# A fused attention, gated MLP and Fourier-mixing kernel: two weight tiles moved among the first q/k tiles, small additions moved to ScalarE

## The chip, the cores and the metric

The kernel runs as one program on one NeuronCore of a Trainium2 chip. The metric is device time in microseconds (us) of one execution; runs are summed up by their median. TensorE is PE in the profile, VectorE is DVE, ScalarE is ACT, GpSimd is POOL and SyncE is SP.

## The reference

The inputs are q, k and v of 4 batches with 8 heads, 512 local and 32 global tokens, and the weights of two MLPs. Each local query sees the 32 global keys and the local keys up to 32 tokens away; each global query sees all keys. Then a gated MLP with a convolution over 3 tokens follows, a Fourier transform over tokens and features, a normalisation, and a second MLP.

```python
def _attn_ref(q_l, k_l, v_l, q_g, k_g, v_g):
    def sm(s):
        s = s - np.max(s, axis=-1, keepdims=True)
        e = np.exp(s)
        return e / (np.sum(e, axis=-1, keepdims=True) + 1e-09)
    ...
    s_g = scale * np.matmul(q_g, k_all.transpose(0, 1, 3, 2))
    out_g = np.matmul(sm(s_g), v_all)
    ...
    s_l = np.concatenate([s_lg, s_ll], axis=-1)
    a_l = sm(s_l)
    out_l = np.matmul(a_l, np.concatenate([v_g, v_l], axis=2))
    return np.concatenate([out_g, out_l], axis=2).astype(np.float32)

def _moe_ref(x, w_in, conv_w, w_out):
    h = np.maximum(x @ w_in, 0.0)
    ...
    gate = 1.0 / (1.0 + np.exp(-conv_out))
    return (h * gate @ w_out).astype(np.float32)

def _moe2_ref(x, w_ch1, w_ch2):
    X = np.fft.fft(np.fft.fft(x, axis=1), axis=2)
    u = x + np.real(X).astype(np.float32)
    ...
    return (u + np.maximum(un @ w_ch1, 0.0) @ w_ch2).astype(np.float32)
```

## The kernel before

The attention goes in 32 units (`for i in range(NU + 2)`), each two heads of one batch and one half of the local queries. A unit's steps are spread over three turns of the loop. In turn i: `s_mm(i)` is eight matmuls for the scores into two banks; `s_max(i)` (L311) adds the mask and takes the row maximum, four DVE instructions with an accumulator read each; `s_exp(i)` (L323) is four exponentials on ScalarE, each with the row sums as its accumulated output in `sm[:, 4:8]`; `s_norm(i)` adds 1e-9 to the four sums (L328), inverts them (L329), and POOL scales the four blocks (L334). In turn i+1 `t_mm` transposes the blocks on PE (L344, L345) and `t_evac` copies them out (L353), half on DVE, half on ScalarE; in turn i+2 `pv_mm` multiplies with v. Units 0 to 3 are the second half of batch 0, units 4 to 7 the first. In turns 5 and 7 of each eight a global softmax stands beside them (`sg_piece`, `pg_soft`, `pg_trans`): two reductions L405, one exponential L415, addition L416, reciprocal L417, scaling on POOL L418, transposes L428 and L429.

The MLP's weights are given as 64-bit floats. For each of 16 tiles (w0 to w7 of the first matrix, w8 to w15 of the second, each 512 KB) `fetch_w` loads the raw words and `make_w` turns them into a pair of 32-bit parts. `from_f64` takes the magnitude on ScalarE (L167), clamps it on POOL (L168), shifts the tail either on ScalarE (L170) or on DVE (L172), and joins the words on DVE (L174, L175). `put` casts on ScalarE (L203) and subtracts on DVE (L204). There are two `mag` buffers, so a third tile waits until the first one's L204 has read its own. The tiles are loaded and made in the order `wq` = w0, w1, w8, w2, w9, w3 and so on; `wsteps` says how many are made in each turn. The first MLP's matmuls begin in turn 6 (`m_g1`).

On SP and PE the order is the program's own (`manual_schedule`). On DVE, ScalarE and POOL the instructions are ordered by the framework's scheduler, with the priorities in `PRIORITY`; a conversion may be issued only after the instruction kept in `last_exp` (`issue_after`). The first weight load has an explicit wait for the matmul `first`. The transfers on SP's queue share eight semaphores in turn, so each waits until the one eight places before it has landed.

Of the kernel before, what the change touches and what calls it, by code (L numbers as in the profile page):

```python
# [128 lines left out]
def fused_kernel(ctx: ExitStack, tc: tile.TileContext, d, out):  # L129
# [186 lines left out]
    @prio("ex")  # L316
    def s_exp(i):
        sm = smalls[i]
        for h in range(2):
            for a in range(2):  # L320
                k = 2 * h + a
                p = pbs(i)[h][:, a, 0:224]
                last_exp[0] = act.activation(p, p, AF.Exp, bias=sm[:, k:k + 1], scale=-1.0, accum_out=sm[:, 4 + k:5 + k])  # L323

    @prio("no")
    def s_norm(i):
        sm = smalls.pop(i)
        dve.tensor_scalar(sm[:, 8:12], sm[:, 4:8], 1e-9, None, op0=ALU.add)  # L328
        dve.reciprocal(sm[:, 12:16], sm[:, 8:12])  # L329
        for h in range(2):  # L330
            for a in range(2):
                p = pbs(i)[h][:, a, 0:224]
                k = 12 + 2 * h + a
                gp.tensor_scalar(p, p, sm[:, k:k + 1], 1.0, op0=ALU.mult, op1=ALU.mult)  # L334
# [76 lines left out]
    def pg_soft(g):  # L411
# [3 lines left out]
        act.activation(s, s, AF.Exp, bias=sm[:, 2:3], scale=-1.0, accum_out=sm[:, 3:4])  # L415
        dve.tensor_scalar(sm[:, 4:5], sm[:, 3:4], 1e-9, None, op0=ALU.add)  # L416
        dve.reciprocal(sm[:, 5:6], sm[:, 4:5])  # L417
# [40 lines left out]
    @prio("w")  # L458
    def make_w(i):
        w = put(wp, f"w{i}", unpack(mp, w_raw.pop(i), gp, i % 2 == 0))  # L460
        (w_in if i < 8 else w_out)[i % 8] = w
# [81 lines left out]
    with tc.manual_schedule(engines={mybir.EngineType.SP, mybir.EngineType.PE}):  # L543
        load_qk(0)
        sp.dma_start(mask[:, 2:4], d["mask"][:, 2:4])
        load_qk(1)
        sp.dma_start(ident, d["ident"])
        load_qk(2)
        for t in pbuf:
# [11 lines left out]
        wq = [0] + [x for m in range(7) for x in (m + 1, 8 + m)] + [15]  # L561
        wsteps = [0, 1, 2, 4, 6, 8, 10, 12, 14, 16]
        fetched = 0
        craw = ap1.tile([128, 24, 2], I32, name="craw")
        cmag = ap1.tile([128, 24], F32, name="cmag")
        for i in range(NU + 2):
# [4 lines left out]
            if live:  # L571
                first = s_mm(i, ("s", "t") if not early or i % 2 == 0 else ("a0", "a1"))
                if i == 0:
                    fetch_w(wq[0], first)
                    load_v(0)
                    sp.dma_start(mask[:, 0:2], d["mask"][:, 0:2])
                    fetched = 1
                while fetched < min(16, (2, 4, 7, 10, 13, 16)[min(i, 5)]):
                    fetch_w(wq[fetched])
                    fetched += 1  # L580
                if i == 1:
                    sp.dma_start(craw.rearrange("p a b -> p (a b)"), bits(d["conv_w"]))
                    gp.dma_start(gmask, d["gmask"])
                s_max(i)
            m_tanh(us[0] - 1)
            if 0 <= i - 2 < NU:
# [395 lines left out]
```

## Time and profile before

| | |
|---|---|
| Runs | 797.38, 797.80, 799.71 us; median 797.8 |
| Profiled execution | 796.53 us; its span 794.6 us |
| PE busy | 765.2 us (96%) |
| DVE busy | 477.9 us (60%) |
| ScalarE busy | 365.1 us (46%) |
| POOL busy | 159.2 us (20%) |
| Moved by the DMA queues | 77.80 MB, mean 98 GB/s |

The span is the time between the first and the last instruction in the trace; the 1.9 us around it belong to the execution's own time. Busy shares are means over stages that differ: in the first 40 us the DMA engines move 311 and then 401 GB/s and PE is little more than half busy; from some 70 us on PE is busy nearly without a gap.

### The profile page before, as it was taken

Reading aid. Unit: us, or ns where it says so; the run is one execution under the profiler, and the core shown is the slowest. Engines: PE = TensorE matmul, PEld = TensorE weight load, DVE = VectorE, ACT = ScalarE, POOL = GpSimd, SP = SyncE. Lnnn points to the kernel's source line nnn. Section 1 sums busy time; section 2 is a strip of 40 time slices with the busy share of each in tenths; the row PEclk is TensorE's granted clock in tenths of the full one; section 3 lists DMA queues with packets and bytes.
Section 4 is the critical chain, followed back from the end, with each engine's and each line's share of the span. In section 5 each row is a group of like instructions: output and inputs, shape, how many; then the busy total and the mean of one; then the engine's idle time right before and its main releaser. Section 6 shows DMA issues by size and latency. Waiting matters only on the chain.

```text
span 794.6 us, 13609 instructions
## 1 busy us (share of the span) xinstructions
PE 765.2 (96%) x5272; PEld 704.4 (89%) x5272; DVE 477.9 (60%) x1167; ACT 365.1 (46%) x884; POOL 159.2 (20%) x213
## 2 busy tenths in 40 slices
PE   6589999999999999999999999999999999999997
PEld 4368989998999988899889999999999999999997
DVE  6999787778777877699775778535422232213113
ACT  6787776777677775545533384313122112211110
POOL 5644423222322221000222022100022012100000
PEclk9889999999999999999999999999999999999999
DMA  8913423442345233436530670020200020001001
GB/s 310 401 45 108 141 79 126 135 168 79 127 134 169 78 111 107 115 114 234 182 102 1 225 254 1 1 91 0 66 26 2 1 90 1 1 1 45 1 1 45
DMA packets 36944, 77.80 MB, mean 98 GB/s; under 512 B 3768, under 2 KB 22072, under 8 KB 36880
## 3 DMA queue, kind: packets, MB, share of 16 engines
q1 hardware_dynamic: 36288, 74.52, 27.0%
q0 software_dynamic: 592, 2.42, 1.2%
q8 instruction: 41, 0.67, 0.3%
q14 instruction: 23, 0.19, 0.1%
HBM read 61.72 MB, written 15.20 MB: 97 GB/s over the span
## 4 chain that ended last, share of the span: by engine, by line
PE 85%; DVE 7%; DMA 3%; ACT 3%; issue 1%; POOL 1%; SPq 0%; DVEq 0%; POOLq 0%; ACTq 0%
PE ps_a L146 34%; PE ps_g L146 23%; PE ps_pv L146 15%; PE ps_s L146 6%; PE ps_t L146 3%; DMA qk<-in_qk_dram 2%; PE ps_s L344 1%; PE ps_t L344 1%; PE ps_s L345 1%; PE ps_t L345 1%; DMA uc<-u_d 1%; ACT pb L323 1%; DVE uc L857 1%; DVE cf L854 1%; DVE mag L174 1%
## 5 line engine op out<-in xcount | busy, mean ns | idle before, releaser
L146 PE MATMUL ps_a<-g,w_w 128*128 128x254 f32 (+1 forms) x768 | 112.7, 295 | 0.2 <-DVE u L541 0.2
L146 PE MATMUL ps_g<-x,w_w 128*128 128x256 f32 (+1 forms) x768 | 111.0, 293 | 1.1 <-ACT h L479 1.1
L146 PEld LDWEIGHTS ps_g<-x,w_w 128*128 128x128 f32 x768 | 100.3, 188 | 6.6 <-issue 4.4
L146 PEld LDWEIGHTS ps_a<-g,w_w 128*128 128x128 f32 x768 | 100.8, 190 | 4.5 <-issue 3.8
L146 PE MATMUL ps_a<-hd,w_w 128*128 128x436 f32 (+1 forms) x480 | 101.4, 360 | 0.0
L334 POOL TENSOR_SCALAR pb<-pb,sm 128x224 f32<-128x224 f32 x128 | 76.1, 613 | 109.2 <-DVE sm L329 42.3
L146 PEld LDWEIGHTS ps_a<-hd,w_w 128*128 128x128 f32 x480 | 90.1, 188 | 4.8
L826 DVE SCALAR_TENSOR_TENSOR hd<-ps_g,hd 128x436 fp32r<-128x436 f32 (+1 forms) x40 | 24.3, 608 | 88.7 <-ACT hd L825 88.7
L168 POOL TENSOR_SCALAR mag<-mag 128x512 f32<-128x512 f32 x48 | 39.6, 827 | 185.0 <-ACT mag L167 183.6
L146 PE MATMUL ps_a<-hd,w_v 128*128 128x436 f32 (+1 forms) x360 | 76.2, 360 | 0.0
L826 DVE SCALAR_TENSOR_TENSOR hd<-ps_pv,hd 128x436 fp32r<-128x436 f32 (+1 forms) x40 | 24.2, 605 | 85.1 <-ACT hd L825 85.1
L825 ACT ACTIVATE hd<-ps_pv 128x436 fp32r<-128x436 f32 (+1 forms) x40 | 21.3, 533 | 115.0 <-PE ps_pv L146 115.0
L825 ACT ACTIVATE hd<-ps_g 128x436 fp32r<-128x436 f32 (+1 forms) x40 | 21.3, 534 | 110.1 <-PE ps_g L146 110.0
L146 PEld LDWEIGHTS ps_a<-hd,w_v 128*128 128x128 f32 x360 | 67.6, 188 | 3.7
L323 ACT ACTIVATE pb<-pb,sm 128x224 f32<-128x224 f32 x128 | 60.4, 473 | 10.6 <-DVE sm L311 10.3
L490 DVE SCALAR_TENSOR_TENSOR y<-h,convw,y 128x254 f32<-128x254 f32 (+1 forms) x64 | 33.7, 527 | 29.0 <-ACT y L489 29.0
L146 PE MATMUL ps_g<-chl,w_w 128*128 128x436 f32 (+1 forms) x240 | 51.0, 361 | 0.0
L146 PE MATMUL ps_s<-qk 64*128 64x224 f32 (+1 forms) x144 | 38.3, 418 | 13.1 <-DMA qk<-in_qk_dram 8.0
L146 PE MATMUL ps_pv<-chl,w_v 128*128 128x436 f32 (+1 forms) x240 | 50.8, 360 | 0.0
L146 PE MATMUL ps_pv<-chl,w_w 128*128 128x436 f32 (+1 forms) x240 | 50.8, 360 | 0.0
L146 PEld LDWEIGHTS ps_pv<-chl,w_v 128*128 128x128 f32 x240 | 45.1, 188 | 2.5
L146 PEld LDWEIGHTS ps_g<-chl,w_w 128*128 128x128 f32 x240 | 44.8, 188 | 2.7 <-issue 0.3
(221 smaller groups left out, 1422.5 us busy)
## 6 DMA issues: line engine op xcount, KB each, us to landing
v<-in_v_dram SPq DMA_DIRECT2D x16, 640.0 KB, 4.9
qk<-in_qk_dram SPq DMA_DIRECT2D x16, 464.0 KB, 5.3
raw_r<-in_ch_dram SPq DMA_DIRECT2D x14, 512.0 KB, 6.2
raw_v<-in_ch_dram SPq DMA_DIRECT2D x13, 512.0 KB, 9.4
kept<-w_o SPq DMA_DIRECT2D x12, 512.0 KB, 3.8
w_w<-kept SPq DMA_DIRECT2D x12, 512.0 KB, 4.4
qk<-in_qk_dram SPq DMA_DIRECT2D x16, 304.0 KB, 4.9
u_d<-u SPq DMA_DIRECT2D x4, 1088.0 KB, 5.2
```

What stands on the lines that cost most here:

```text
L146: return pe.matmul(o, a, b, start=start, stop=stop)
L168: (clamp or dve).tensor_scalar(mag, mag, TOP, 2.0, op0=ALU.min, op1=ALU.max)
L174: dve.scalar_tensor_tensor(val, val, 3, tail, op0=ALU.logical_shift_left, op1=ALU.bitwise_or)
L323: last_exp[0] = act.activation(p, p, AF.Exp, bias=sm[:, k:k + 1], scale=-1.0, accum_out=sm[:, 4 + k:5 + k])
L334: gp.tensor_scalar(p, p, sm[:, k:k + 1], 1.0, op0=ALU.mult, op1=ALU.mult)
L344: pe.transpose(tb[:, 128 * a:128 * a + 128], pb[:, a, 0:128], ident)
L345: pe.transpose(tb[:, 256 + 128 * a:384 + 128 * a], pb[:, a, 128:256], ident)
L490: dve.scalar_tensor_tensor(y, hb[:, cc - 1:cc - 1 + n], convw2[:, m, 0:1], y, op0=ALU.mult, op1=ALU.add)
L825: act.activation(hd[:, 0], o, AF.Relu)
L826: dve.scalar_tensor_tensor(hd[:, 1], o, 0.0, f32(hd[:, 0]), op0=ALU.max, op1=ALU.subtract)
L854: dve.tensor_mul(tmp[:, e], acc[e], rs_t[c])
L857: dve.tensor_add(o, o, tmp[:, e])
```

## The change

The change does five things.

1. The loads of q/k tiles 1 and 2 and of the identity move behind unit 0's scores in the program, and w0 and w1 are loaded among them: w0 ahead of q/k tile 1, w1 ahead of q/k tile 2. w0's load loses its wait for the matmul.
2. w0 is made in turn 0, right behind `s_max(0)`, without the `issue_after`; `wsteps` is moved accordingly, so one more tile is made by the end of turns 0 to 5 (two more in turn 1), and the same number from turn 6 on.
3. w0's tail is shifted on DVE (L172) and no longer on ScalarE (L170).
4. The addition of 1e-9 to a unit's sums is a Copy with a bias on ScalarE (L324 of the changed kernel), issued behind the four exponentials, and it is what `last_exp` keeps.
5. The same for the global softmax (L416).

```diff
--- before.py
+++ after.py
@@ -320,12 +320,12 @@
             for a in range(2):
                 k = 2 * h + a
                 p = pbs(i)[h][:, a, 0:224]
-                last_exp[0] = act.activation(p, p, AF.Exp, bias=sm[:, k:k + 1], scale=-1.0, accum_out=sm[:, 4 + k:5 + k])
+                act.activation(p, p, AF.Exp, bias=sm[:, k:k + 1], scale=-1.0, accum_out=sm[:, 4 + k:5 + k])
+        last_exp[0] = act.activation(sm[:, 8:12], sm[:, 4:8], AF.Copy, bias=1e-9)
 
     @prio("no")
     def s_norm(i):
         sm = smalls.pop(i)
-        dve.tensor_scalar(sm[:, 8:12], sm[:, 4:8], 1e-9, None, op0=ALU.add)
         dve.reciprocal(sm[:, 12:16], sm[:, 8:12])
         for h in range(2):
             for a in range(2):
@@ -413,7 +413,7 @@
         s = sg4s[g % 2][:, 0:KC]
         dve.tensor_tensor(sm[:, 2:3], sm[:, 0:1], sm[:, 1:2], op=ALU.min)
         act.activation(s, s, AF.Exp, bias=sm[:, 2:3], scale=-1.0, accum_out=sm[:, 3:4])
-        dve.tensor_scalar(sm[:, 4:5], sm[:, 3:4], 1e-9, None, op0=ALU.add)
+        act.activation(sm[:, 4:5], sm[:, 3:4], AF.Copy, bias=1e-9)
         dve.reciprocal(sm[:, 5:6], sm[:, 4:5])
         gp.tensor_scalar(s, s, sm[:, 5:6], 1.0, op0=ALU.mult, op1=ALU.mult)
 
@@ -457,7 +457,7 @@
 
     @prio("w")
     def make_w(i):
-        w = put(wp, f"w{i}", unpack(mp, w_raw.pop(i), gp, i % 2 == 0))
+        w = put(wp, f"w{i}", unpack(mp, w_raw.pop(i), gp, i % 2 == 0 and i > 0))
         (w_in if i < 8 else w_out)[i % 8] = w
 
     g_t, acc = {}, {}
@@ -543,9 +543,6 @@
     with tc.manual_schedule(engines={mybir.EngineType.SP, mybir.EngineType.PE}):
         load_qk(0)
         sp.dma_start(mask[:, 2:4], d["mask"][:, 2:4])
-        load_qk(1)
-        sp.dma_start(ident, d["ident"])
-        load_qk(2)
         for t in pbuf:
             dve.memset(t[:, :, 224:256], 0.0)
         for t in sg4s:
@@ -559,7 +556,7 @@
         NU = B * H
         glob = {8 * b + 5 + 2 * k: 2 * b + k for b in range(B) for k in range(2)}
         wq = [0] + [x for m in range(7) for x in (m + 1, 8 + m)] + [15]
-        wsteps = [0, 1, 2, 4, 6, 8, 10, 12, 14, 16]
+        wsteps = [1, 2, 4, 5, 7, 9, 11, 12, 14, 16]
         fetched = 0
         craw = ap1.tile([128, 24, 2], I32, name="craw")
         cmag = ap1.tile([128, 24], F32, name="cmag")
@@ -571,10 +568,14 @@
             if live:
                 first = s_mm(i, ("s", "t") if not early or i % 2 == 0 else ("a0", "a1"))
                 if i == 0:
-                    fetch_w(wq[0], first)
+                    fetch_w(wq[0])
+                    load_qk(1)
+                    sp.dma_start(ident, d["ident"])
+                    fetch_w(wq[1])
+                    load_qk(2)
                     load_v(0)
                     sp.dma_start(mask[:, 0:2], d["mask"][:, 0:2])
-                    fetched = 1
+                    fetched = 2
                 while fetched < min(16, (2, 4, 7, 10, 13, 16)[min(i, 5)]):
                     fetch_w(wq[fetched])
                     fetched += 1
@@ -582,6 +583,8 @@
                     sp.dma_start(craw.rearrange("p a b -> p (a b)"), bits(d["conv_w"]))
                     gp.dma_start(gmask, d["gmask"])
                 s_max(i)
+                if i == 0:
+                    make_w(wq[0])
             m_tanh(us[0] - 1)
             if 0 <= i - 2 < NU:
                 pv_mm(i - 2, "pv" if not early or (i - 2) // 2 % 2 == 0 else "g1")
```

What the order of instructions shows. SP's queue from its start (`raw_w0` is the raw tile of w0, and so on), before and then now:

```order
L273 DMA qk_103<-in_qk_dram 128x608
L545 DMA mask_86<-in_mask_dram 128x448
L273 DMA qk_106<-in_qk_dram 128x608
L547 DMA ident_85<-in_ident_dram 128x128
L273 DMA qk_109<-in_qk_dram 128x608
L182 DMA raw_w0_135<-in_w_in_dram 128x4x256
L280 DMA v_137<-in_v_dram 128x1280
L576 DMA mask_86<-in_mask_dram 128x448
L182 DMA raw_w1_140<-in_w_in_dram 128x4x256
```

```order
L273 DMA qk_103<-in_qk_dram 128x608
L545 DMA mask_86<-in_mask_dram 128x448
L182 DMA raw_w0_130<-in_w_in_dram 128x4x256
L273 DMA qk_132<-in_qk_dram 128x608
L573 DMA ident_85<-in_ident_dram 128x128
L182 DMA raw_w1_135<-in_w_in_dram 128x4x256
L273 DMA qk_137<-in_qk_dram 128x608
L280 DMA v_139<-in_v_dram 128x1280
L577 DMA mask_86<-in_mask_dram 128x448
```

w0 stands ahead of the second q/k tile, w1 ahead of the third; both v and the second half of the mask come behind all of them.

DVE from its first waiting instruction on (`pb` and `sm` are a unit's block and its row statistics), before and then now:

```order
L311 ISA pb0_90,sm_142<-ps_s_129,mask_86 128x224
L311 ISA sm_142 128x1
L311 ISA pb0_90,sm_142<-ps_s_129,mask_86 128x224
L311 ISA sm_142 128x1
L311 ISA pb1_91,sm_142<-ps_t_130,mask_86 128x224
L311 ISA sm_142 128x1
L311 ISA pb1_91,sm_142<-ps_t_130,mask_86 128x224
L311 ISA sm_142 128x1
L328 TENSOR_SCALAR sm_142<-sm_142 128x4
L329 RECIPROCAL sm_142<-sm_142 128x4
```

```order
L172 TENSOR_SCALAR raw_w0_130<-raw_w0_130 128x512
L311 ISA pb0_90,sm_142<-ps_s_124,mask_86 128x224
L311 ISA sm_142 128x1
L311 ISA pb0_90,sm_142<-ps_s_124,mask_86 128x224
L311 ISA sm_142 128x1
L311 ISA pb1_91,sm_142<-ps_t_125,mask_86 128x224
L311 ISA sm_142 128x1
L311 ISA pb1_91,sm_142<-ps_t_125,mask_86 128x224
L311 ISA sm_142 128x1
L172 TENSOR_SCALAR raw_w1_135<-raw_w1_135 128x512
L174 SCALAR_TENSOR_TENSOR mag_147<-mag_147,raw_w0_130 128x512
L329 RECIPROCAL sm_142<-sm_142 128x4
```

The tail of w0 stands ahead of unit 0's reductions; w1's tail and w0's first join stand between them and unit 0's reciprocal, and the addition is gone.

DVE around the first global softmax (`sg0`, `smg`) and unit 6 (the block `pb0`), before and then now:

```order
L204 TENSOR_TENSOR w_w10_428<-mag_422,w_w10_428 128x512
L174 SCALAR_TENSOR_TENSOR mag_431<-mag_431,raw_w4_296 128x512
L405 ISA sg0_88,smg_494<-ps_s_491,gmask_87 128x304
L405 ISA smg_494 128x1
L172 TENSOR_SCALAR raw_w7_446<-raw_w7_446 128x512
L175 SCALAR_TENSOR_TENSOR mag_431<-raw_w4_296,mag_431 128x512
L405 ISA sg0_88,smg_494<-ps_t_496,gmask_87 128x304
L405 ISA smg_494 128x1
L414 TENSOR_TENSOR smg_494<-smg_494 128x1
L204 TENSOR_TENSOR w_w4_437<-mag_431,w_w4_437 128x512
L174 SCALAR_TENSOR_TENSOR mag_509<-mag_509,raw_w11_298 128x512
L311 ISA pb0_90,sm_533<-ps_s_527,mask_86 128x224
```

```order
L204 TENSOR_TENSOR w_w4_437<-mag_431,w_w4_437 128x512
L204 TENSOR_TENSOR w_w11_446<-mag_440,w_w11_446 128x512
L405 ISA sg0_88,smg_503<-ps_s_500,gmask_87 128x304
L405 ISA smg_503 128x1
L405 ISA sg0_88,smg_503<-ps_t_505,gmask_87 128x304
L405 ISA smg_503 128x1
L414 TENSOR_TENSOR smg_503<-smg_503 128x1
L311 ISA pb0_90,sm_542<-ps_s_536,mask_86 128x224
L311 ISA sm_542 128x1
L311 ISA pb0_90,sm_542<-ps_s_536,mask_86 128x224
L311 ISA sm_542 128x1
L174 SCALAR_TENSOR_TENSOR mag_518<-mag_518,raw_w5_309 128x512
```

Before, L204 of w4 and L174 of w11 stand between the second reduction L405 and unit 6's first; now both reductions stand together, behind the L204 of w4 and w11, and unit 6 follows at once.

## Rows read from the trace of the kernel before

**Rows 1.** The stages: us, busy time of each engine, granted clock of PE, DMA share, GB/s.

```profile
0.00:13.00 13.00, 7.63 (x34) 4.89 (x36) 5.20 (x38) 6.82 (x20) 4.30 (x15) 1.00 0.79 263
13.00:42.60 29.60, 17.81 (x130) 12.38 (x128) 28.86 (x85) 22.12 (x59) 21.39 (x28) 0.85 1.01 390
42.60:51.02 8.42, 8.38 (x57) 6.99 (x59) 7.44 (x23) 8.00 (x21) 3.71 (x5) 0.70 0.01 4
51.02:69.69 18.67, 16.00 (x165) 13.29 (x165) 18.67 (x55) 15.94 (x45) 9.57 (x12) 1.00 0.34 115
69.69:294.00 224.31, 224.31 (x2079) 205.47 (x2080) 175.48 (x548) 162.06 (x462) 64.07 (x109) 1.00 0.36 119
294.00:345.00 51.00, 48.12 (x451) 44.98 (x450) 36.92 (x88) 28.46 (x69) 6.86 (x12) 1.00 0.33 97
```

**Rows 2.** PE's waits up to 70.5 us: total, times, longest.

```profile
PE ps_s L146 <- DMA qk<-in_qk_dram: 8.0, 2, 4.3
PE ps_s L146 <- DVE smg L405: 5.1, 2, 4.3
PE ps_s L428 <- POOL sg L418: 1.2, 1, 1.2
```

**Rows 3.** The chain of waits: start, us, what.

```profile
42.64 0.74 PE ps_t L146
67.65 1.99 POOL sg L418
```

**Rows 4.** Timeline of DVE: start, us, instruction, idle time before it.

```profile
42.12 0.46 DVE L405 CUSTOM_DVE_ANT_0 sg<-ps_t,gmask 128x304 f32<-128x304 f32 x1
44.09 0.38 DVE L311 CUSTOM_DVE_ANT_0 pb<-ps_s,mask 128x224 f32<-128x224 f32 x1
51.02 0.39 DVE L311 CUSTOM_DVE_ANT_0 pb<-ps_a,mask 128x224 f32<-128x224 f32 x1 [0.52 <-PE ps_a L146]
67.26 0.15 DVE L328 TENSOR_SCALAR sm<-sm 128x4 f32<-128x4 f32 x1
67.33 0.15 DVE L417 RECIPROCAL smg<-smg 128x1 f32<-128x1 f32 x1
```

**Rows 5.** Timeline of SP's DMA issues.

```profile
1.66 0.42 SPq L273 DMA_DIRECT2D qk<-in_qk_dram  x1
5.61 0.38 SPq L182 DMA_DIRECT2D raw_w<-in_w_in_dram  x1
```

**Rows 6.** Timeline of ScalarE: the first passes over w0 and w1.

```profile
8.99 0.68 ACT L167 ACTIVATE mag<-raw_w 128x512 f32<-128x512 f32 x1 [1.01 <-DMA raw_w<-in_w_in_dram]
13.37 0.69 ACT L167 ACTIVATE mag<-raw_w 128x512 f32<-128x512 f32 x1 [0.81 <-DMA raw_w<-in_w_in_dram]
```

**Rows 7.** The sixth to eighth us, columns as in rows 1.

```profile
5.00:6.00 1.00, 0.54 (x4) 0.00 (x0) 0.42 (x3) 0.00 (x0) 0.00 (x0) 1.00 0.73 272
6.00:7.00 1.00, 0.66 (x4) 0.62 (x6) 0.91 (x6) 0.99 (x5) 0.00 (x0) 1.00 0.32 96
7.00:8.00 1.00, 1.00 (x8) 0.56 (x4) 0.00 (x0) 0.98 (x5) 0.00 (x0) 1.00 1.01 342
```

**Rows 8.** Timeline of POOL: unit 0 is scaled.

```profile
8.59 1.76 POOL L334 TENSOR_SCALAR pb<-pb,sm 128x224 f32<-128x224 f32 x4 [5.91 <-DVE sm L329]
```

**Rows 9.** ScalarE's groups up to 80 us: count, busy us, mean ns, idle before.

```profile
L167 ACT ACTIVATE cmag<-craw 128x24 f32<-128x24 f32 x1 | 0.2, 207 | 0.0
```

**Rows 10.** DVE's groups up to 80 us, columns as in rows 9.

```profile
L172 DVE TENSOR_SCALAR raw_w<-raw_w 128x512 int32<-128x512 int32 x8 | 3.9, 485 | 0.0
L174 DVE SCALAR_TENSOR_TENSOR mag<-mag,raw_w 128x512 int32<-128x512 int32 x16 | 11.2, 701 | 0.4 <-POOL mag L168 0.4
L175 DVE SCALAR_TENSOR_TENSOR mag<-raw_w,mag 128x512 int32<-128x512 int32 x16 | 11.6, 723 | 0.1
L204 DVE TENSOR_TENSOR w_w<-mag,w_w 128x512 fp32r<-128x512 f32 x15 | 10.5, 698 | 0.2
L353 DVE COPY pt<-ps_s 128x512 f32<-128x512 f32 x5 | 3.4, 680 | 0.3 <-PE ps_s L345 0.3
```

## The prediction

> **What bounds the kernel now.** I read the stages first [rows 1]. From 69.69 us to 294 us PE is busy for 224.31 of 224.31 us, so in that stage nothing on another engine costs time; there and later PE's own work is fixed, and the change adds no matmul. Ahead of it PE has 49.8 us of work in 69.69 us. What can move is the moment when the unbroken run begins, which I call the mark. The list of PE's waits up to there [rows 2] shows on what PE stood: 8.0 us on q/k tiles (4.3 us in one wait) and 5.1 us on the first global softmax's reduction (4.3 us in one). Its last wait, 1.2 us, ends at the mark and is in the chain of waits [rows 3]: POOL's L418 (67.65 us) scales the second global softmax, and it is held by DVE's reciprocal L417, issued at 67.33 us [rows 4]. So the question is when DVE reaches that L417.
>
> DVE is what runs late. From 13.00 to 42.60 us it is busy 28.86 of 29.60 us, from 51.02 to the mark all the time; only ahead of 13 us it is idle, 13.00 - 5.20 = 7.8 us [rows 1]. Between 42.64 and 51.02 us the chain runs through PE instead (unit 6's scores, then its neighbours, unit 7's scores, then DVE's L311 at 51.02 us) [rows 3, 4]. PE's granted clock is 0.70 in the mean over these 8.42 us [rows 1]: 60% of them, 5.1 us, at the lower of its two levels (1.2 of 2.4 GHz), behind its long wait for that reduction.
>
> **The transfers.** The first weight tile, w0, is issued at 5.61 us, behind PE's first matmuls [rows 5], and w1 after it. ScalarE's first pass over them starts at 8.99 and 13.37 us, each ending a wait for the tile [rows 6]. Meanwhile the DMA engines moved 272 GB/s in the sixth us and 96 in the seventh [rows 7], against 390 in the full stage after 13 us [rows 1]. With the tiles ahead this hole of (390 - 272) + (390 - 96) = 412 KB is filled: worth 412 KB / 390 GB/s = 1.1 us to every later transfer. But the longest wait for a q/k tile isn't shortened by as much, since PE then waits for late transposes (below).
>
> When does w0 come? It takes the slot in which the second q/k tile is issued now, 1.66 us [rows 5]. The first q/k tile (304 KB), the mask (112 KB) and the global mask (152 KB) go before, then 512 KB: 1080 KB, from about 2 us on at 272 GB/s or a bit over, 4.0 us: **about 6.0 us instead of 8.99**. Then q/k tile 1 (304 KB), the identity (64 KB) and w1 (512 KB) at 342 GB/s, as in the eighth us [rows 7]: **w1 at 8.6 instead of 13.37**. q/k tile 1 is pushed back by w0 to about 7 us, q/k tile 2 by w1 to about 9.5 and the first v tile to about 11; the last two are wanted only behind unit 0's transposes, which follow POOL's first scaling (8.59 us [rows 8] now, later in the new order). Everything behind them on SP's queue has the same bytes ahead of it as before, and no wait for PE's first matmuls.
>
> **The change, term by term**, as shifts of L417 against 67.33 us.
>
> (1) The small additions. Ahead of L417 DVE loses nine L328 and two L416. One takes 0.15 us, but its successor starts 0.07 us behind it when it doesn't depend on it (67.26 to 67.33) [rows 4]. So 11 x 0.07 = 0.8 us at least and 11 x 0.15 = 1.7 us at most; the row is from DVE's busy stage, where nearly all of them lie, so **-0.8**. ScalarE gets eleven Copies; the nearest row is 0.207 us (128x24) [rows 9], 2.3 us in all. It is idle for 29.60 - 22.12 = 7.5 us of the second stage and 2.7 us of the last [rows 1], which covers them: 0.
>
> The Trainium skill says the opposite of what this part does: "ScalarE: Activation LUTs", Rules for kernel authors, gives additions to VectorE and not to ScalarE. By it the term would be a loss, and the time the second rival's.
>
> (2) What stands ahead of L417 in DVE's new order: one L172 more (w0's tail, which was ScalarE's L170), one L204 more, one copy of a transposed block (L353) less: 0.485 + 0.698 - 0.680 [rows 10] = **+0.5**.
>
> (3) The early idle. The new order opens with w0's L172, so DVE stands until 6.0 us (5.2 us idle, since its memsets take 0.8), does that and unit 0's four reductions (1.7 us), stands for w1 until 8.6 us (0.9 us) and is then full: 6.1 us idle instead of 7.8. The gain is 1.7 at most. It isn't had whole, since ScalarE and POOL hold DVE at new places: POOL clamps both tiles before it scales unit 0 (8.59 us now, then about 10.3, with w1's tile at 8.6 and the two passes over it), and the cast of w1 stands behind two passes over w8. At least it is 0. Half of it: **-0.9**.
>
> (4) The reductions of the first global softmax. Ahead of the second of them DVE has more to do than before: two L172, one L174, one L175 and two L204, less six L328. By their means [rows 10] 0.97 + 0.70 + 0.72 + 1.40 = 3.8, less 0.08 for the overlap of each = 3.3, less 6 x 0.07 = 2.9. With (3) the second reduction moves from 42.12 to about 44.1 us, **2.0 late**. PE's unit 6 waits for exactly this, and so the stretch through PE, 42.64 to 51.02, begins 2.0 late. Now DVE fills 1.5 us until unit 6's scores are there (42.12 + 0.46 = 42.58 to 44.09 [rows 4]) with L204 and L174; in the new order it goes to unit 6 at once and stands. The stretch itself stays at 8.4 us or gets shorter by what the clock gives back: 5.1 us of it are at the lower clock, so 0 to 2.5 us; PE stands ahead of it in the new order too, so I stay near the lower end and take 0.6. Unit 7's reductions then start at 51.02 + 2.0 - 0.6 = 52.4.
>
> (5) From unit 7's reductions to L417 DVE now needs 67.33 - 51.02 = 16.3 us. In the new order one L174, one L175 and one L353 less stand there, and one L204 more, since they were done before: -0.70 - 0.72 - 0.68 + 0.70 = -1.4, and -0.1 with the overlap and the three additions (in (1) already): **-1.5**. L417 comes at 52.4 + 16.3 - 1.5 = 67.2. PE, which has 16.00 us of work in that stage [rows 1], would be ready at 52.4 + 16.0 = 68.4, so the POOL wait still decides.
>
> **The sum**: terms (1) and (2) lie inside (4) and (5), which count every instruction ahead of L417; so the mark moves by 2.0 - 0.6 - 1.5 = -0.1 us. DVE's and ScalarE's orders differ up to the last softmaxes; around them PE has 2.9 us of waits from 294 to 345 [rows 1], so this may bring -1 to +0.5; I take 0. Span 794.5, the profiled execution 796.53 - 0.1 = 796.4. The median of the runs is 797.8, 1.3 us above that execution: **797.7 us, no change that can be told**. Told apart can be 0.3%, about 2.4 us: under 795.4 and over 800.2.
>
> **The rivals.**
> - *The early fill pays (faster).* (3) gives its 1.7 whole, and PE's stretch escapes the lower clock (2.5 instead of 0.6): -0.1 - 0.8 - 1.9 = -2.8, **795.0**. For it speaks that DVE has no other slack and that w0 surely comes earlier; against it that the same transfers and the same order make units 2 to 5 later, which keeps PE idle ahead of 42 us as it is now. Chance 0.31.
> - *The additions are dearer on ScalarE.* Where ScalarE has the next word, each Copy costs 0.21 where DVE gave back 0.07: 11 x 0.14 = +1.5, **799.2**; this ends within 0.3%. It holds if ScalarE has no idle time left between 13 us and the mark; the rows give it 10 us. Chance 0.07. This is where the rule of the Trainium skill's page on ScalarE, above, would lead.
> - *The conversions stand in the units' way (slower).* The two tiles are ahead of unit 0 on DVE, ScalarE and POOL, and each following unit inherits it. If (3) gives nothing, (4) is 2.9 late, the clock gives nothing back and (5) still returns 1.5, the mark is 1.4 late; with one more wait of 1.2 for ScalarE's casts it is 2.6, **800.4**. It decides if the second global reduction starts after 45.0 us. For it speaks that unit 0's scaling alone comes 1.7 late in (3) and that a unit's transposes stand ahead of the next unit's on PE; against it that DVE's total work ahead of the mark is no larger. Chance 0.17.
> - The forecast itself has 0.45.
>
> **How the numbers follow.** Faster 0.31, slower 0.17, within 0.3% the rest, 0.52. The range reaches to the first rival's time and the last one's, 794.8 to 800.3. The forecast's own range, with (3) from 0 to -1.7, is 796.9 to 798.6.
>
> **What would show it.** Right: ScalarE's first pass over w0 at about 6 us, w1's at 9 to 10; unit 0's scaling on POOL 1.5 to 2 us late; the second global reduction between 43.5 and 45 us, with a DVE wait of about 1.3 behind it; the Copies at 0.2 us without ScalarE idle falling away; PE's last wait within 1 us of 69.7. Wrong: a mark moved by over 2 us, PE at full clock through unit 6, or new PE waits after 70 us.

## The result, and the profile after

The changed kernel takes 802.9 us in the median (801.6 to 804.9) against 798.7 for the kernel before beside it: a ratio of 1.0053, with an interval of 1.0034 to 1.0072. It is 4.2 us slower; the forecast was 797.7 with a range up to 800.3, and slower had a chance of 0.17. The profiled execution took 803.45 us, its span 801.1.

The stages, with the borders and columns of [rows 1]:

```profile
0.00:13.00 13.00, 3.72 (x16) 2.36 (x17) 5.29 (x36) 6.10 (x17) 3.66 (x13) 1.00 0.84 283
13.00:42.60 29.60, 22.14 (x144) 14.62 (x144) 28.34 (x80) 24.64 (x70) 21.34 (x28) 0.88 0.89 339
42.60:51.02 8.42, 5.79 (x33) 4.85 (x33) 6.91 (x21) 5.48 (x15) 3.04 (x6) 0.61 0.38 150
51.02:69.69 18.67, 15.59 (x148) 12.35 (x146) 17.69 (x52) 15.14 (x42) 7.27 (x12) 0.87 0.32 103
69.69:294.00 224.31, 223.94 (x2063) 205.39 (x2064) 171.86 (x510) 164.34 (x487) 75.08 (x108) 1.00 0.36 120
```

Ahead of 69.69 us PE worked 47.2 us (before 49.8), and the stage from 51.02 us, at full clock before, was granted 0.87. Behind it there is next to no change. The granted clock of 1.00 in the first row, here and in [rows 1], is not what the matmuls show: PE's transposes (L345, 128x128) take 0.42 us each up to 10.7 us before and up to 20.3 us now, as they do where the granted clock is at its lower level, and 0.27 us from 14.3 and 20.7 us on. So PE stays at the lower level longer than before at the start; what this costs was not told apart. PE takes its matmuls in the same order in all kernels here, so the k-th can be compared: the 481st started at 79.56 us before and 6.1 us later now, the 4901st 6.5 us later. The loss is made ahead of 80 us.

PE's waits up to 80 us (total, times, longest), against [rows 2]:

```profile
PE ps_s L146 <- DVE smg L405: 7.2, 2, 4.6
PE ps_a L344 <- POOL pb L334: 5.8, 7, 2.5
PE ps_s L146 <- DMA qk<-in_qk_dram: 3.7, 1, 3.7
PE ps_a L146 <- DMA qk<-in_qk_dram: 3.1, 1, 3.1
```

The wait for GpSimd's L418, on which the prediction rested, is gone. Both global softmaxes' reductions were waited for already; the wait for the second pair grew from 0.8 to 2.6 us. The waits for the scaled blocks, 2.0 us before, come to 5.8.

The start, as the timelines of DVE and POOL show it:

```profile
7.84 0.43 DVE L172 TENSOR_SCALAR raw_w<-raw_w 128x512 int32<-128x512 int32 x1 [6.25 <-DMA raw_w<-in_w_in_dram]
8.18 0.38 DVE L311 CUSTOM_DVE_ANT_0 pb<-ps_s,mask 128x224 f32<-128x224 f32 x1
10.15 0.43 DVE L172 TENSOR_SCALAR raw_w<-raw_w 128x512 int32<-128x512 int32 x1 [0.64 <-DMA raw_w<-in_w_in_dram]
...
18.68 0.38 DVE L311 CUSTOM_DVE_ANT_0 pb<-ps_s,mask 128x224 f32<-128x224 f32 x1
```

```profile
8.63 0.61 POOL L168 TENSOR_SCALAR mag<-mag 128x512 f32<-128x512 f32 x1 [5.94 <-ACT mag L167]
11.47 0.61 POOL L168 TENSOR_SCALAR mag<-mag 128x512 f32<-128x512 f32 x1 [2.23 <-ACT mag L167]
12.18 3.87 POOL L334 TENSOR_SCALAR pb<-pb,sm 128x224 f32<-128x224 f32 x5
```

w0 landed at 7.8 us and w1 at 10.1, not at 6.0 and 8.6. Unit 0's reductions follow at 8.18 us, its scaling on POOL at 12.18 us (8.59 before [rows 8]; forecast 10.3). Unit 2's reductions start at 18.68 us.

The later places, from DVE's timeline, against [rows 4]:

```profile
45.10 0.46 DVE L405 CUSTOM_DVE_ANT_0 sg<-ps_t,gmask 128x304 f32<-128x304 f32 x1
47.13 0.39 DVE L311 CUSTOM_DVE_ANT_0 pb<-ps_s,mask 128x224 f32<-128x224 f32 x1 [0.93 <-PE ps_s L146]
54.33 0.39 DVE L311 CUSTOM_DVE_ANT_0 pb<-ps_a,mask 128x224 f32<-128x224 f32 x1 [0.66 <-PE ps_a L146]
64.40 0.46 DVE L405 CUSTOM_DVE_ANT_0 sg<-ps_s,gmask 128x304 f32<-128x304 f32 x1
68.12 0.38 DVE L311 CUSTOM_DVE_ANT_0 pb<-ps_s,mask 128x224 f32<-128x224 f32 x1
69.36 0.15 DVE L417 RECIPROCAL smg<-smg 128x1 f32<-128x1 f32 x1
```

Unit 8's reductions (68.12 us here) stood in DVE's timeline before at

```profile
63.49 0.38 DVE L311 CUSTOM_DVE_ANT_0 pb<-ps_s,mask 128x224 f32<-128x224 f32 x1
```

Between the first two of the rows above PE's timeline has unit 6's scores:

```profile
45.23 0.74 PE L146 MATMUL ps_s<-qk 64*128 64x224 f32 x1 [4.60 <-DVE smg L405]
45.62 0.74 PE L146 MATMUL ps_t<-qk 64*128 64x224 f32 x1
```

The second reduction of the first global softmax is 3.0 us late (45.10 against 42.12), unit 6's scores in the second bank start at 45.62 us against 42.64 [rows 3], unit 7's reductions are 3.3 us late (54.33 against 51.02), the L417 2.0 (69.36 against 67.33). But PE no longer waits for what L417 releases: unit 8's scores wait 2.6 us for the L405 of 64.40, and PE goes on at 64.92 us at its lower clock, as two stretches of the same profile show:

```profile
60.00:64.92 4.92, 2.32 (x49) 1.56 (x49) 4.92 (x12) 3.31 (x8) 4.21 (x5) 1.00 0.32 92
64.92:71.82 6.90, 6.90 (x34) 5.41 (x35) 6.22 (x22) 5.71 (x18) 1.39 (x1) 0.51 0.73 244
```

6.9 us at a granted clock of 0.51 do the work of 3.5 at the full one.

### The profile page after: what moved, and what is told of

Its sections match the earlier page's. It is cut to its first block, busy times and chain, and to the rows that moved or that the text cites. A ratio compares the mean times of both kernels' runs of the same rounds, so it can differ in the third digit from the quotient of the medians.

```text
span 801.1 us, 13573 instructions
## 1 busy us (share of the span) xinstructions
PE 768.9 (96%) x5272; PEld 706.9 (88%) x5272; DVE 476.7 (60%) x1128; ACT 370.2 (46%) x923; POOL 168.3 (21%) x213
## 4 chain that ended last, share of the span: by engine, by line
PE 82%; DVE 9%; ACT 3%; DMA 2%; POOL 1%; issue 1%; SPq 0%; DVEq 0%; POOLq 0%; ACTq 0%
PE ps_a L146 33%; PE ps_g L146 22%; PE ps_pv L146 15%; PE ps_s L146 5%; PE ps_t L146 3%; DVE mag L174 1%; ACT pb L323 1%; POOL pb L334 1%; DVE mag L175 1%; DVE pb L311 1%; DMA raw_w<-in_w_in_dram 1%; PE ps_t L344 1%; DMA uc<-u_d 1%; PE ps_t L345 1%; PE ps_s L344 1%
## 5 line engine op out<-in xcount | busy, mean ns | idle before, releaser
L334 POOL TENSOR_SCALAR pb<-pb,sm 128x224 f32<-128x224 f32 x128 | 88.9, 711 | 52.5 <-DVE sm L329 31.2
L168 POOL TENSOR_SCALAR mag<-mag 128x512 f32<-128x512 f32 x48 | 36.0, 749 | 247.0 <-ACT mag L167 189.3
L497 ACT ACTIVATE y<-y 128x254 f32<-128x254 f32 (+1 forms) x64 | 27.6, 431 | 47.6 <-DVE y L491 47.4
```

Of the source, the lines that this page charges most:

```text
L168: (clamp or dve).tensor_scalar(mag, mag, TOP, 2.0, op0=ALU.min, op1=ALU.max)
L497: act.activation(g_t[u], g_t[u], AF.Tanh, scale=0.5)
```

## The experiments

Two theories stood at the start: that w0's tail at the head of VectorE's queue holds the units (head of line), and that the megabyte ahead of q/k tiles 1 and 2 does (transfers). The additions were the third. All runs in one table; "conversions" are the L172, L174, L175 and L204 on the 16 weight tiles ahead of unit 8's first reduction (L311) in VectorE's order, "unit 8" is the start of that reduction in us, "work" and "idle" are VectorE's busy and idle time from 0 up to it, and "PE" is the shift of the 481st matmul against the kernel before.

```
run        median  ratio to before           conversions  unit 8  work  idle   PE
before      798.1                                   45    63.5   54.0   9.5    0
changed     802.9  1.0053 (1.0034..1.0072)          49    68.1   56.7  11.5  +6.1
e1_loads    807.3  1.0114 (1.0095..1.0132)          45    69.1   55.9  13.2 +10.3
e2_adds     796.4  0.9978 (0.9968..0.9988)          42    60.7   50.8   9.9  -4.0
e3          803.5  1.0072 (1.0051..1.0093)          49    67.9   57.4  10.5  +6.2
e4          799.6  1.0019 (1.0005..1.0033)          42    64.0   51.2  12.8  +1.5
f1          800.1  1.0025 (1.0010..1.0039)          45    64.6   54.0  10.6  +1.1
f2          800.6  1.0040 (1.0026..1.0054)          45    63.4   53.3  10.1  -0.6
f3          800.9  1.0040 (1.0026..1.0054)          45    65.0   53.3  11.7  +1.1
f4          804.6  1.0085 (1.0065..1.0105)          49    68.5   56.0  12.5  +6.6
g1          808.6  1.0120 (1.0099..1.0141)          49    71.1   57.2  13.8  +8.8
g2          803.3  1.0058 (1.0040..1.0076)          46    67.8   53.5  14.3  +3.8
h1          799.2  1.0015 (1.0002..1.0028)          42    61.2   50.8  10.3  +1.4
k1          797.6  0.9994 (0.9981..1.0008)          45    63.7   54.3   9.4  +0.2
p1          803.1  1.0054 (1.0041..1.0068)          49    69.0   56.3  12.7  +5.5
p2          802.7  1.0053 (1.0038..1.0068)          49    68.0   56.1  11.9  +4.5
p3          798.6  1.0004 (0.9992..1.0016)          45    64.9   54.1  10.8  +1.4
p4          798.6  0.9998 (0.9987..1.0010)          45    64.2   53.2  11.0  +0.2
p5          806.0  1.0100 (1.0081..1.0118)          46    63.1   52.5  10.6  +7.1
p6          797.4  0.9995 (0.9983..1.0007)          41    61.5   50.2  11.3  -2.0
```

(The kernel before had medians of 797.6 to 798.8 beside the several runs; the ratios are to the one beside. The other columns are of one profiled execution each. Two nearly equal kernels, the one before and k1, differ in them by 0.2 to 0.3 us. Whole executions differ by more: those of the kernel before took 795.7 to 801.5 us, at mean granted clocks of 0.981 to 0.994, and its profiled one, 796.53 us at 0.991, is among the shorter.)

### The parts, with the scheduler free

**e1_loads**: part 1 alone (the hunks of the diff at lines 543 and 571).

> Part 1 of the change alone: w0 and w1 are loaded among the q/k tiles, without the wait for a matmul; conversions are started where they were, additions are on VectorE. Theory 'head of line' (the loss is made by w0's L172, which stands ahead of unit 0's reductions on VectorE and holds them until w0 lands at 7.84 us): unit 0's reductions start at 5.6 us again, POOL's first scaling within 1 us of 8.6, and the time is within 1.5 us of the kernel before (797.2 to 800.2). Theory 'transfers' (the loss is made by the 1 MB of weights that stand ahead of q/k tiles 1 and 2; unit 1's scores 8.62 instead of 6.34): unit 1 starts at 8.6 us here too, the second reduction of the first global softmax starts 2 us or more later than 42.12, and the time is 801 to 804. Theory 'additions' (the Copy on ScalarE behind each unit's exponentials makes every unit later): same as before, 798 to 799.5.

**e2_adds**: parts 4 and 5 alone (the hunks at lines 320 and 413).

> Parts 4 and 5 alone: the additions of 1e-9 are Copies on ScalarE; loads, conversions and w0's tail as in the kernel before. Theory 'additions': slower by 2 us or more (over 800.7), with VectorE waiting for the Copy ahead of the reciprocals of the first units, each unit 0.2 us or more later than before. Theories 'head of line' and 'transfers': no loss from this part; 797 to 799.5, or up to 0.8 us faster by the VectorE time that goes.

**e3_loads_make**: all but the hunks of the additions.

> Parts 1 to 3 without the additions: the loads are moved, w0 is made in turn 0 ahead of unit 0's exponentials, its tail is on VectorE. Theory 'head of line': the whole loss is here, 801 to 804, with unit 0's reductions behind L172 at about 8.2 us. Theory 'transfers': the same 801 to 804, so this run tells these two apart only beside the run with the loads alone. Theory 'additions': within 1.5 us of the kernel before.

**e4_loads_adds**: all but these lines of the change:

```diff
-        w = put(wp, f"w{i}", unpack(mp, w_raw.pop(i), gp, i % 2 == 0 and i > 0))
+        w = put(wp, f"w{i}", unpack(mp, w_raw.pop(i), gp, i % 2 == 0))
-        wsteps = [1, 2, 4, 5, 7, 9, 11, 12, 14, 16]
+        wsteps = [0, 1, 2, 4, 6, 8, 10, 12, 14, 16]
-                if i == 0:
-                    make_w(wq[0])
```

> The whole change without parts 2 and 3: loads moved and additions on ScalarE, but w0 and the others made in the turns of the kernel before and w0's tail on ScalarE. Theory 'head of line': the loss is gone, 796.5 to 799.5, and unit 0's reductions start at 5.6 us. Theory 'transfers': 801 to 804 in spite of that. Theory 'additions': 801 or more, as in the run with the additions alone.

No theory fits all four, and e1's 807.3 lies above what any of them named. The loads alone cost 9 us, with the additions beside them 1.5, and the additions alone gain 1.7: the parts don't add up, since each makes the scheduler order VectorE, ScalarE and GpSimd anew. In e1 and e4 the new order put w1's L172, which waits for its tile until 9.9 us, ahead of unit 0's reciprocal. So the order had to be held.

### The parts, in a given order

In these kernels a list gives the places of all instructions of the three engines, tied by edges that set the order and wait for nothing:

```diff
         fused_kernel(tc, d, out)
+        set_order(nc, tc)
...
+        for a, b in zip(seq, seq[1:]):
+            tc.add_manual_dep(
+                own[b], own[a].name,
+                mybir.DependencyInfo(mybir.DependencyClass.NoSync, mybir.DependencyReason.DATA), reason="order",
+            )
```

**f1_loads_order_before, f2_adds_order_before, f3_loads_adds_order_before**: e1, e2 and e4 in the order of the kernel before. **f4_after_unit0_first**: the changed kernel in its own order, with unit 0's steps ahead of w0's and w1's.

> The loads moved alone (part 1), while VectorE, ScalarE and GpSimd take every instruction in exactly the order of the kernel before (written out as ordering edges). The run with the loads alone, whose order the scheduler had chosen anew, took 807.3 us, 9.2 more than before. Theory 'order' (the loads cost little; what costs is the order of conversions and units that the scheduler picks for them, with instructions that wait for a weight tile ahead of unit 0's): 796.5 to 799.7. Theory 'transfers' (unit 1 is held at 8.4 us instead of 6.3 by 1 MB of weights ahead of q/k tiles 1 and 2, and the shift stays): unit 1's scores at 8.4, unit 2's more than 1.5 us later than 11.02, and the time 800 to 803, whatever the order.

> The additions on ScalarE alone (parts 4 and 5), every other instruction of VectorE, ScalarE and GpSimd in exactly the order of the kernel before, each Copy right behind its exponential. The run with the additions alone and an order of the scheduler's own was 1.7 us faster than before (796.4). Theory 'additions help by themselves' (VectorE ahead of 67 us loses 11 instructions of 0.07 to 0.15 us): 796.5 to 797.6. Theory 'order' (the gain there came from the order): 797.7 to 798.8, no difference that can be told.

> Loads moved and additions on ScalarE (parts 1, 4 and 5), in the order of the kernel before on the three engines. With the scheduler's own order it was 799.6. Theory 'order': 796 to 799, near the sum of the two runs beside this one. Theory 'transfers': 799.5 to 803.

> The whole change in its own order, but for 8 places at the start: unit 0's four reductions and its reciprocal stand ahead of the tails of w0 and w1 on VectorE, its exponentials ahead of w0's first pass on ScalarE, its scaling ahead of both clamps on GpSimd. Theory 'head of line' (w0's and w1's instructions ahead of unit 0's make the loss): unit 0's reductions at 5.6, scaling at about 8.6 us, unit 0's transposes at 9.1 instead of 13.0, the second reduction of the first global softmax 2 us or more earlier than 44.8, time 796.5 to 799.5. Theory 'order further on' (the loss comes from later places of the new order, such as conversions among units 2 to 5): unit 0 is early again and the gain is gone by 45 us; 801 to 803.5. Theory 'transfers': unit 1's scores stay at 8.6 and the time at 800 to 803.

In one order the parts can be read. The loads alone cost 2.4 us, not 9.2: 1.1 of it is VectorE's new idle time ahead of unit 8 (10.6 against 9.5), since unit 1's scores wait for their tile until 7.8 us instead of 6.3; in its profile most of the rest comes at 327 us, where f1's PE has a spell at the lower clock that the profile of before has not:

```profile
326.90:330.40 3.50, 3.50 (x18) 3.50 (x17) 1.42 (x4) 0.89 (x3) 0.00 (x0) 0.51 0.01 0
```

Whether that spell belongs to f1 or to the one execution is not shown: p3's profile has it too (328.2 us), and p3 as a whole is as fast as the kernel before. The time, 800.1, is where "transfers" had it, but the sign of that theory is missing: unit 2's reductions are only 0.2 us late in f1 (13.23 against 13.02) and 0.9 in f3.

The additions do ahead of 80 us what term (1) said: 0.7 us less work up to unit 8, PE 0.6 us ahead. But PE loses 2.0 us again between 80 and 300 us, in steps of 0.15 to 0.25 with hardly a wait in the list (f3 loses the same 2.0), and 1.5 us in such a spell at 328 us; f2's 800.6 is above what either theory had. Head of line falls with f4: unit 0's transposes began 2.7 us earlier than in the changed kernel and ended 4.0 us earlier, 12 us later PE was 1.2 us behind it, and the 804.6 is above what any theory had.

**g1_start_before, g2_start_after**: the changed kernel with the order of before up to unit 3 and its own behind it, and the reverse.

> The whole change, with the order on VectorE, ScalarE and GpSimd up to unit 3's first instruction that of the kernel before (7 instructions of conversions on VectorE instead of 17 ahead of unit 3's reductions) and that of the changed kernel from there. Theory 'early conversions' (the loss is made in the first 25 us, where w0's to w4's conversions stand ahead of units 0 to 2: unit 2's reductions at 18.7 instead of 13.0 us): units 2 and 3 early again, PE ahead of 100 us within 2 us of the kernel before, time 797 to 801. Theory 'later places' (the order behind unit 3 makes it): 801.5 to 804.5.

> The mirror image: the whole change, with its own order up to unit 3's first instruction and the order of the kernel before from there. Theory 'early conversions': 801.5 to 805, PE 4 us or more late by 45 us and still so at 100 us. Theory 'later places': 798 to 801, the early shift of 5 us made good before 70 us.

Both theories fail in g1. Cut at unit 3, the conversions that the first part left out all come up right there: 17 stand ahead of unit 3's reductions in g1 as in the changed kernel (6 in the one before), and PE waits 7.5 us in one piece for the copy L353 behind them. A good start is worth nothing if the work follows in one lump. g2 went as "early conversions" had it: the start alone leaves 3.8 us at 80 us, all of it idle time (4.8 us more up to unit 8, with 0.5 us less work).

**h1_early_adds** and **k1_no_wait_order_before** change the kernel before:

```diff
-                    fetch_w(wq[0], first)
+                    fetch_w(wq[0])
```

is k1; in h1 the Copies stand under `if i < 9` and `if g < 2`, the additions of the others on VectorE, in the order of e2 up to unit 9 and of the kernel before from there.

> Loads of the kernel before; the additions on ScalarE for the first nine units and two global softmaxes only, on VectorE for the others; the order of the run with the additions alone (796.4) up to unit 9 and that of the kernel before from there. That run was 4.1 us ahead at 72 us and gave 1.9 us back behind it; the run with the additions in the old order was 0.9 us ahead there and gave back 2.3 us up to 310 us in steps of 0.1 to 0.2. Theory 'order early, additions late' (the gain is the early order's, the late loss is the Copies' on ScalarE): 3.5 to 4 us faster, 793.5 to 795. Theory 'given back anyway' (whoever is early at 72 us waits later, whatever the additions): 796 to 797.5.

> The kernel before, order of all engines and of the loads unchanged, but w0's load without its wait for the first scores. The run with the loads moved, in the same order, was 2.4 us slower, with unit 1's scores at 8.4 instead of 6.3 us. Theory 'pushed back' (what costs there is the megabyte ahead of q/k tiles 1 and 2): nothing is pushed back here, 796.5 to 798.3. Theory 'no wait' (more loads at once slow every one of them): q/k tile 1 later than 6.6 us, 799 or more.

k1: the missing wait costs nothing, so f1's idle time is the pushed-back tiles'. h1: the postponed conversions come in one lump at unit 9 (PE waits 5.2 us for L311, and 2.9 us ahead becomes 1.4 us late); but from 80 to 299 us it loses 0.1 us where f2 lost 2.0, so f2's late loss is the late Copies'. The 799.2 misses both theories, by the lump.

### Which wait, or how much work

**p1_second_early, p2_both_early, p3_before_both_early, p4_early_adds_both_early** move only the L405s in the given order: the second pair, or both, ahead of conversions and MLP steps.

> The changed kernel in its own order, but for two instructions on VectorE: the two reductions of the second global softmax (L405) stand seven and eight places earlier, right behind the unit's second L491, ahead of L174, L204, L490, L508 and L450. Theory 'reduction held' (unit 8's scores wait until 64.92 for these reductions, PE then stands 2.6 us, falls to the lower clock for 65.0 to 71.8 us and loses 3.4 us more): the reductions start at 62.0 to 62.5, unit 8's scores before 63, no spell at the lower clock behind 60 us, PE's work at 80 us 3 to 4 us earlier, time 798.5 to 800. Theory 'total' (VectorE's sum of work sets the end, whichever instruction is first): GpSimd's scaling L418 of that softmax ends no earlier than 71 us, PE waits for it instead, time 801.5 to 803.5.

> As the run beside it, and the two reductions of the first global softmax stand eight places earlier too, ahead of L175, L174, L175, the copy L353, L172, L390 and two L204 (4.3 us of work). Theory 'reduction held': unit 6's scores start at about 41 instead of 45.2, unit 7's reductions 3 us or more before 54.3, time 795 to 798. Theory 'total': the mark stays where the first run has it, within 1 us; time within 1 us of it.

> The kernel before in its own order, but for the reductions of the global softmaxes on VectorE: the first pair stands right behind the seventh tile's L175 (nine and twelve places earlier, 37.4 instead of 40.4 and 42.1 us), the second pair together. Theory 'reduction held': PE's wait for them falls from 4.3 to about 1.5 us, unit 6's scores 3 us or more earlier; the mark itself follows by as much as VectorE had idle time between 42.6 and 51 us, 1 us, so 796.3 to 797.3. Theory 'total': 797.5 to 798.5, no difference.

> The same two pairs moved in the order of the kernel before, and the additions on ScalarE for the first nine units and two global softmaxes, on VectorE for the others. The additions alone in that order were 0.9 us ahead at 72 us and lost 2.3 us between 80 and 310 us, which the run with early additions alone did not lose. Theory 'reduction held' and 'late additions cost': 0.9 us less than the run beside it, 795.3 to 796.5. Theory 'total': 796.8 to 797.8.

The waits went where they were sent, and the time stayed: p1 and p2 have the changed kernel's ratio, though in their profiles PE is 0.6 and 1.6 us less late at 80 us. In p2 unit 6's scores start at 41.1 us, 0.2 us from the kernel before, and unit 8's scores wait for nothing; then its list of waits from 35 us has

```profile
PE ps_s L344 <- DVE sm L311: 2.4, 1, 2.4
```

unit 7's transposes, whose bank is free when unit 8's reductions (67.98 us, 68.12 in the changed kernel) have read it. The list of p1 has the same row; it is not the L418 that "total" expected there. In its claim that the time stays "total" holds, within what the intervals can tell (some 1.2 us), in p3 and p4 too.

**p5_unit8_early** moves unit 8's four reductions up as well. **p6_later_steps** is the changed kernel in the scheduler's order, with

```diff
-        wsteps = [1, 2, 4, 5, 7, 9, 11, 12, 14, 16]
+        wsteps = [1, 1, 2, 3, 5, 7, 9, 11, 13, 16]
```

> The changed kernel's order with both pairs of global reductions early (the run that took 802.7), and on VectorE unit 8's four reductions moved up as well, behind the second pair, L414 and two conversions: ahead of three conversions (1.9 us), seven instructions of the MLP and the global softmax (2.6 us). In that run unit 7's transposes waited 2.4 us for unit 8's reductions (68.0 us). Theory 'place' (what is ahead of unit 8's reductions decides): they start at about 64 us, the 2.4 us go, PE at 80 us is 2 to 3 us earlier and the time 799.5 to 801. Theory 'total' (the work that is passed over is wanted as well): the MLP's steps L491, L508, L510 come later, PE's matmuls wait for them instead, and the time is 802 to 803.5.

> The changed kernel with the weight tiles made later: wsteps of 1, 1, 2, 3, 5, 7, 9, 11, 13, 16 instead of 1, 2, 4, 5, 7, 9, 11, 12, 14, 16; loads, w0 in turn 0, its tail and the additions as in the change. The scheduler then puts 41 conversion instructions ahead of unit 8's reductions on VectorE, against 49 in the changed kernel and 45 in the one before, each about 0.6 us. Theory 'total ahead of unit 8' (VectorE's work and idle time up to there set the end; over the runs the shift of unit 8's reductions and of PE at 80 us agree within 1.5 us): unit 8's reductions 8 times 0.6 = 4.8 us earlier than 68.1 us if the idle time stays, 63 to 65 us, and 797.5 to 800. Theory 'start' (the loss is w0's and w1's loads and conversions ahead of units 0 and 1, which are still there): 801.5 to 803.5.

In p5 the reductions come 5 us earlier, and PE then waits for the MLP, whose steps were passed over; its list from 56 us holds one line, and the time, 806.0, is 3 us worse and above what either theory had:

```profile
PE ps_g L146 <- ACT h L479: 5.3, 2, 4.8
```

p6 takes work away from that place instead. VectorE up to unit 8's first reduction (us, busy, granted clock of PE, DMA share, GB/s), in the kernel before, the changed one, and p6 (whose nearest stretch ends at 61.50 us):

```profile
0.00:63.49 63.49, 53.98 (x180) 0.89 0.69 256
```

```profile
0.00:68.12 68.12, 56.66 (x176) 0.88 0.66 241
```

```profile
0.00:61.50 61.50, 50.20 (x167) 0.94 0.73 269
```

With the early loads, w0's conversion in turn 0, its tail on VectorE and the additions all kept, VectorE's work up to unit 8 is 6.5 us shorter: 8 conversions fewer (5.7 us) and two steps of the MLP fewer (L491, L508; 1.4 us). Its idle time is the same (11.3 against 11.5 us), unit 8 comes 6.7 us earlier and the whole kernel is as fast as before (0.9995). Its time, 797.4, lies 0.1 us below what "total" expected; "start" is 4 us off. So the work that the table `wsteps` puts ahead of unit 8 decides, in a stage where VectorE has no time left. But p6 is not the change with the old table: at the end of the turns 2 to 7 it has one tile fewer made than the kernel before, two fewer than the changed one at the end of the turns 1 to 5. Nearest to the old table is e4, which also has w0 made later and its tail on ScalarE; it is still 0.19% slower than before, against 0.53%. And of the 4.6 us by which unit 8 is late in the changed kernel, 2.7 us are work (conversions 3.2 us and MLP steps 1.2 us more, additions 1.4 us less) and 2.0 us idle time, which comes with the early loads (1.1 us more in f1, 2.2 in f3). The larger part of the loss goes with the earlier conversions, then, and the rest with the idle time, which the additions and the later steps together can pay for. The scheduler's new order comes with the table and can't be told from it here.

**Faster than both** is e2 alone, the additions in the scheduler's order, by 0.22% (0.12 to 0.32%), again with fewer conversions ahead of unit 8 (42).

**Open** is why e1 is 4.7 us later at 80 us than its unit 8 accounts for (+10.3 against +5.6): PE waits 6.6 us in all between 60 and 95 us, and from 82.3 us it has a stretch of 3.4 us at a granted clock of 0.50, which is 1.7 us; what brings the waits was not tried. Open too is what starts the spells at the lower clock near 327 us in some profiles and not in others, and by what path the late Copies hold PE.

## Why the prediction was wrong

- **What bounds the kernel: right.** VectorE's lateness ahead of some 70 us decides, and nothing behind it does, but for the late Copies, which I took at 0: 2.0 us in f2; in the changed kernel PE loses 0.4 us between 80 and 240 us, where e3, without Copies, loses nothing.
- **The transfers and (3), the early idle time: wrong in sign.** The step that failed is "1080 KB, from about 2 us on": it lets w0 land when the bytes ahead of it are through. The rate came as estimated, 271 GB/s in the mean up to w0's landing at 7.84 us:

```profile
2.00:4.00 2.00, 0.32 (x2) 0.33 (x4) 0.00 (x0) 0.02 (x1) 0.69 (x5) 1.00 0.89 248
4.00:6.00 2.00, 1.54 (x8) 0.85 (x6) 0.00 (x0) 0.00 (x0) 0.00 (x0) 1.00 0.81 239
6.00:8.00 2.00, 0.00 (x0) 0.00 (x0) 0.16 (x1) 0.16 (x1) 0.00 (x0) 1.00 1.05 332
```

  From 2 us to w0's landing that is 496 + 478 + 1.84 x 332 = 1585 KB, half a megabyte more than stands ahead of it: the transfers issued behind w0 ran beside it. Forecast were 1.7 us less idle time at most and 0 at least; it became 0.6 us more up to unit 2's reductions (18.68 - 10.32 = 8.4 us, before 13.02 - 5.22 = 7.8) and 2.0 more up to unit 8's.
- **(1) right**: 0.7 us less work where -0.8 was said (f2). That is a small reading, since k1, with the work of the kernel before, has 0.3 us more. The rule of the Trainium skill ("ScalarE: Activation LUTs", Rules for kernel authors: additions to VectorE) is borne out in its sign where the order is held: the Copies cost 0.40% there (f2). In e2 they stand in a new order with three conversions fewer ahead of unit 8, and its gain of 0.22% can't be put down to them.
- **(2) and (4) right in kind**: the first global softmax's second reduction came 3.0 us late instead of 2.0, the stall behind it was there (0.93 us, and 1.5 more up to unit 7's reductions). The clock took instead of giving: the stretch from there through PE lasted 8.7 us (45.62 to 54.33), where 8.4 - 0.6 = 7.8 were said; PE was busy all through both stretches, at a granted clock of 0.67 now and 0.70 before.
- **(5) is the step that failed.** Its sum held: from unit 7's reductions to L417 VectorE needed 15.0 us, 1.3 less than before, -1.5 was said. But L417 was the wrong place to count to. Ahead of it stand two conversions more than before (49 against 47), as (2) had it; ahead of unit 8's reductions, which precede it, four more (49 against 45), 2.4 us by some 0.6 each. "PE would be ready at 52.4 + 16.0, so the POOL wait still decides" took PE's work of that stage as one piece that can start at once; it goes through unit 8's scores and reductions, which were 4.6 us late, and the wait ahead of them put PE on the lower clock for 6.9 us. A sign of it stood in the trace before: of the 5.1 us in [rows 2], which the prediction gave to the first global softmax, 0.8 are PE's wait for the second pair of reductions, ahead of unit 8's scores:

```profile
59.71 0.64 PE L146 MATMUL ps_s<-qk 64*128 64x224 f32 x2 [0.78 <-DVE smg L405]
60.65 0.45 PE L146 MATMUL ps_t<-qk 64*128 64x224 f32 x1 [0.30 <-DVE smg L405]
```

- **The rival "the conversions stand in the units' way"** came nearest: conversions ahead of the units, and its point, the second reduction later than 45.0 us (45.10). Where it put the cause, at unit 0, f4 does not bear it out. Its 800.4 is 2.5 us short, by the clock and by (5), which it took over; 0.9 us of that are the kernel before itself, which ran at 798.7 beside the changed one and not at 797.8. What the prediction held against it was that VectorE's work ahead of the mark is no larger: ahead of unit 8, where it counts, it is 2.7 us larger (56.7 against 54.0).
- The range, given as 794.8 to 800.3, should by the prediction's own rivals reach from 795.0 to 800.4.

## What to carry to other kernels

Where one engine is full for a whole stage, count all its work up to each thing that the other engines wait for, and not only up to the last wait of the old trace: work that is done earlier there is work put ahead of something. Moving single instructions in such a queue moved the wait and not the end here (p1 to p5); less work ahead moved the end (p6). And where a scheduler sets the order, test a part of a change in the old order too, or the order's effect passes for the part's.

## What was not expected of the hardware

- A transfer did not land here when the bytes ahead of it in its queue were through: w0, third in the queue and issued at 1.66 us, took 6.2 us, while 0.5 MB issued behind it moved as well (rows above).
- GpSimd's scaling of a 128x224 block takes 0.44 us while VectorE works on L311 (1.76 us for unit 0's four [rows 8]) and up to 1.40 us beside the conversions: in the changed kernel unit 0's four took 3.4 us, from 12.18 to 15.60 (the fifth in the row above is unit 1's). The Trainium skill, "SBUF — State Buffer", Who interferes with whom, says that a VectorE instruction with two SBUF inputs contends with a GpSimd instruction that reads SBUF; L174, L175 and L204 have two, and the trace agrees. For unit 0's four blocks that is 1.7 us, just where PE waited for them.
- A wait of 2.6 us ahead of dense matmuls cost PE another 3.4 us through the clock (6.9 us at 0.51), more than the wait itself. In p2 a wait of 2.4 us was followed by 3.4 us at 0.50, which is 1.7 us.
